# A gated recurrence followed by a max-of-two feed-forward layer: opening reordered, weights prepared in quarters, first casts released chunk by chunk

## The chip, the cores and the metric

The kernel runs on one core of one Trainium2 chip. The metric is the device time of one execution in microseconds (us). A core has these engines: TensorE (PE in the profile; its weight loads are listed apart as PEld), VectorE (DVE), ScalarE (ACT), GpSimd (POOL) and SyncE (SP), which here issues DMAs. Each engine runs its own instructions in program order and waits at semaphores for the others.

## The reference

```python
# x, f_logit: (4, 6144, 256); lower_bound: (256,); all float32
sig = 1.0 / (1.0 + np.exp(-f_logit))
f = lower_bound + (1.0 - lower_bound) * sig
i = 1.0 - f
for t in range(S):                       # S = 6144, h starts at 0 for each of the 4 sequences
    h = f[:, t] * h + i[:, t] * x[:, t]
    y[:, t] = h
X = y.reshape(24576, 256)
g = np.maximum(X @ w1, X @ w2)           # w1, w2: (256, 1024)
out = g @ w_out                          # w_out: (1024, 256)
```

## The kernel before, in words

**Algebra.** With u = sigmoid(-f_logit) and om = 1 - lower_bound, f is 1 - om u and i is om u. The kernel scans y' = f y' + u x, so that y = om y', and puts om into the weights. max(a, b) is a + relu(b - a); so the layer becomes out = relu(y' wd) w_out + y' w13, with wd = om (w2 - w1) and w13 = om (w1 w_out). Both are made in the kernel's opening. Everything that feeds PE is bf16.

**Blocks and chunks.** The 24576 tokens are 48 blocks of 512 (`TB`), 12 to a sequence. Blocks 0 to 2 are loaded as float32 rows, go through sigmoid (`gate_nat`) and product (`drive_nat`) and are transposed by PE (`turn_pe`). All later blocks come in chunks: chunk 0 is block 3 alone, chunk 1 is blocks 4 and 5, chunk 2 is 6 and 7, and so on. `cast(c)` (line 172) has POOL issue two DMAs, fs and xs, that cast the chunk's f_logit and x to bf16 into DRAM scratch; there are `NS` = 3 scratch pairs, taken in turn. `turn_dma(c)` (line 184) has SP issue two DMA transposes from scratch to SBUF, fT and xT. Then `gate(b)` on ACT makes u (line 189), `drive(b)` on DVE makes v = u x (line 200), and for each of the two halves h of the 256 channels DVE makes ff = 1 - om u (`forget`, line 135) and scans (`scan`, line 148).

**The layer.** `hidden(j, fc)` (line 220) makes one of eight groups of 128 hidden units of block j: two matmuls 128x512, one for each half of the channels, into a PSUM tile dT of a pool of five, and a relu that takes it to SBUF as rt, on ACT (line 232) or DVE (line 230). `project(j, slot)` (line 251) is a piece of five matmuls 128x256 into psO (a pool of three): eight steps with rt and w_out, and two with y' and w13. `store` evacuates psO on DVE (line 267) and has SP store it (line 269).

**Order.** It is written out by hand; nothing is planned by a scheduler. In the loop over j (line 466), group fc of block j alternates on PE with a piece of the projection of block j - 1. `gate_at` tells at which (j, fc) the instructions of a block's gate, product and scans are issued: block 3 at (2, 2), 4 at (3, 1), 5 at (3, 5), and b at (b - 2, 4) after that. `turn_of` tells where a chunk's transposes are issued: chunk 0 at (1, 5), 1 at (2, 6), and c at three blocks ahead of its first, group 5. After turn_dma(c) stands cast(c + NS), which waits until its scratch pair was read. SP's one queue holds the loads, then stores and transposes in that order; a transpose that waits holds the stores behind it.

**Opening (lines 366 to 464).** SP issues the loads of blocks 0 to 2 and of the weights, the latter in quarters of w1 and w2 (`weight_load`) and halves of w_out (`wout_load`); ACT issues a first piece of x and lower_bound. PE runs matmuls on a tile of zeros (`keep_warm`). Block 0 is done in two halves of 256 tokens. The weights are prepared in two halves of 512 hidden units: `diff(g)` subtracts on DVE (line 301), `scale(g)` multiplies by om on ACT (line 308), `turn_w1` transposes w1 on PE (line 315), `keep_w1` copies that to SBUF on ACT (line 321), POOL casts w_out to bf16 (lines 423 and 431), and `linear_weights` makes w13 (lines 330 and 339). The eight groups of block 0, its projection and block 1 are woven in between. Then a copy on POOL (line 462) waits for the last load of block 2, and cast(0), cast(1) and cast(2) follow at once.

**Hidden units in a group.** `unit(fc)` takes every fourth of 512 columns; so the weights that PE loads for a group of `wd`, and the columns of w1 that it transposes, lie four elements apart. w_out's rows are loaded to match: one partition gets four rows that follow each other, 4 KB in one piece.

Of the kernel before, what the change touches and what calls it, by code (L numbers as in the profile page):

```python
# [8 lines left out]
FP32 = mybir.dt.float32  # L9
BF16 = mybir.dt.bfloat16  # L10
ALU = mybir.AluOpType
# [5 lines left out]
def kernel(  # L17
# [28 lines left out]
    chunks = [(NP, 1)] + [(j, CB) for j in range(NP + 1, NBLK, CB)]  # L46
    NCH = len(chunks)
    home = {j + o: (c, o) for c, (j, n) in enumerate(chunks) for o in range(n)}
    NS = 3

    const = ctx.enter_context(tc.tile_pool(name="const", bufs=1))
    wpool = ctx.enter_context(tc.tile_pool(name="wpool", bufs=1))
# [155 lines left out]
    HF = DFF // 2  # L208

    def unit(fc):  # L210
        g, q = divmod(fc, 4)
        return slice(g * HF + q, (g + 1) * HF, 4)

    rts = {}

    def hidden(j, fc, on_dve=False):
        y = ys[j]
        dT = ps_d.tile([P, TB], FP32, name="dT")
        for kc in range(KC):
            nc.tensor.matmul(  # L220
                dT[:],
                lhsT=wd[:, kc, unit(fc)],
                rhs=y[:, kc, :],
                start=(kc == 0),
                stop=(kc == KC - 1),
            )
        rt = rpool.tile([P, TB], BF16, name="rt")
        rts[j, fc] = rt
        if on_dve:
            nc.vector.tensor_relu(out=rt[:], in_=dT[:])  # L230
        else:
            nc.scalar.activation(out=rt[:], in_=dT[:], func=AF.Relu)  # L232

    pos = {}

# [51 lines left out]
    def weight_load(k, w, src):  # L287
        cols = slice(k * QF, (k + 1) * QF)
        nc.sync.dma_start(
            out=w[:, :, cols], in_=src[:, cols].rearrange("(h p) f -> p h f", p=P)  # L290
        )

    def wout_load(g):
        nc.sync.dma_start(
            out=won[:, 4 * g : 4 * g + 4, :],
            in_=moe_w_out[g * HF : (g + 1) * HF, :].rearrange("(p q) c -> p q c", q=4),
        )

    def diff(g, eng):
        cols = slice(g * HF, (g + 1) * HF)  # L300
        eng.tensor_tensor(
            out=wdf[:, :, cols], in0=w2n[:, :, cols], in1=w1n[:, :, cols], op=ALU.subtract
        )

    def scale(g):
        cols = slice(g * HF, (g + 1) * HF)
        for h in range(KC):
            nc.scalar.activation(
                out=wd[:, h, cols], in_=wdf[:, h, cols], func=AF.Copy, scale=om[:, h : h + 1]
            )  # L310

    def turn_w1(g, h):
        pt = ps_d.tile([P, TB], FP32, name="dT")
        for q in range(4):
            nc.tensor.transpose(
                pt[:, q * P : (q + 1) * P], w1n[:, h, unit(4 * g + q)], ident[:]
            )
        return pt

    def keep_w1(g, h, pt):  # L320
        nc.scalar.copy(
            out=w1T[:, 4 * g : 4 * g + 4, h * P : (h + 1) * P],
            in_=pt[:].rearrange("p (q d) -> p q d", q=4),
        )

    def linear_weights():
        psw = ps_o.tile([P, 2, D], FP32, name="psO")
        for h in range(KC):
            for fc in range(FC):
                nc.tensor.matmul(  # L330
                    psw[:, h, :],
                    lhsT=w1T[:, fc, h * P : (h + 1) * P],
                    rhs=wob[:, fc, :],
                    start=(h == 0 and fc == 0),
                    stop=(h == 1 and fc == FC - 1),
                    skip_group_check=True,
                )
        for h in range(KC):
            nc.scalar.mul(w13[:, h, :], psw[:, h, :], om[:, h : h + 1])

    idle = ps_o.tile([P, 2, D], FP32, name="psO")

# [7 lines left out]
                stop=True,  # L350
            )

    gate_at = {NP: (2, 2), NP + 1: (3, 1), NP + 2: (3, 5)}
    gate_at |= {b: (b - 2, 4) for b in range(NP + 3, NBLK)}
    gate_of = {}
    for b, at in gate_at.items():
        gate_of.setdefault(at, []).append(b)
    turn_of = {(1, 5): 0, (2, 6): 1}
    turn_of |= {(chunks[c][0] - 3, 5): c for c in range(2, NCH)}

    with tc.manual_schedule():
        for j in range(NP):
            alloc_in(j)


        load(0, 0, 0, 2)
        load(0, 1, 0, 2, nc.scalar)
        nc.scalar.dma_start(out=lbc[:], in_=lower_bound.rearrange("(h p) -> p h", p=P))
        for k in range(2):
            weight_load(k, w1n, moe_w1)  # L370
            weight_load(k, w2n, moe_w2)
# [4 lines left out]
        for k in range(2, 4):  # L376
            weight_load(k, w1n, moe_w1)
            weight_load(k, w2n, moe_w2)
        wout_load(1)
        for q0 in (0, 2):  # L380
            for s in range(2):
                load(1, s, q0, q0 + 2)
        for s in range(2):
            load(2, s, 0, NQ)

        nc.vector.memset(warm[:], 0.0)  # L386
        make_identity(nc, ident[:])
        nc.vector.tensor_copy(out=ident_b[:], in_=ident[:])
        keep_warm(9)


        gate_nat(0, 0, 2)
        drive_nat(0, 0, 2)
        for s in range(2):
            for q in range(2):
                turn_pe(0, s, q)
        nc.vector.tensor_scalar(
            out=om[:], in0=lbc[:], scalar1=-1.0, scalar2=1.0, op0=ALU.mult, op1=ALU.add
        )
        nc.vector.tensor_scalar_add(out=nom[:], in0=lbc[:], scalar1=-1.0)  # L400
        for h in range(KC):
            forget(0, h, 0, HB, on_act=True)
        for h in range(KC):
            scan(0, h, 0, HB)
        keep_warm(3)
        gate_nat(0, 2, 4)
        drive_nat(0, 2, 4)
        for s in range(2):
# [1 line left out]
                turn_pe(0, s, q)  # L410
        for h in range(KC):
            forget(0, h, HB, TB, on_act=True)
        diff(0, nc.vector)
        scale(0)
        pts = [turn_w1(0, h) for h in range(KC)]
        for h in range(KC):
            scan(0, h, HB, TB)
        keep_warm(3)
        for q in range(4):
            hidden(0, q, on_dve=(q % 2 == 1))  # L420
        for h in range(KC):
            keep_w1(0, h, pts[h])
        nc.gpsimd.tensor_copy(out=wob[:, 0:4, :], in_=won[:, 0:4, :])
        for i in range(4):
            project_steps(0, i, 0, 4)
        diff(1, nc.vector)
        scale(1)
        pts = [turn_w1(1, h) for h in range(KC)]
        for q in range(4):
            hidden(0, 4 + q, on_dve=(q % 2 == 1))  # L430
        nc.gpsimd.tensor_copy(out=wob[:, 4:8, :], in_=won[:, 4:8, :])
        for h in range(KC):
            keep_w1(1, h, pts[h])


        gate_nat(1, 0, 2)
        drive_nat(1, 0, 2)
        linear_weights()
        for s in range(2):
            for q in range(2):  # L440
                turn_pe(1, s, q)
# [3 lines left out]
            scan(1, h, 0, HB)  # L445
        gate_nat(1, 2, 4)
        drive_nat(1, 2, 4)
        for i in range(2):
            project_steps(0, i, 4, 8)
        for s in range(2):  # L450
            for q in range(2, 4):
                turn_pe(1, s, q)
# [1 line left out]
            forget(1, h, HB, TB, on_act=True)  # L454
        for h in range(KC):
            scan(1, h, HB, TB)
        for i in range(2, 4):
            project_steps(0, i, 4, 8)
        for i in range(4):
            project_steps(0, i, 8, 10)  # L460

        nc.gpsimd.tensor_copy(out=held[:], in_=ins[2][1][:, NQ - 1, D - 1 : D])
        for c in range(NS):
            cast(c)

        for j in range(1, NBLK + 1):
            if j == 2:
                for slot in range(4):
                    project(1, slot)
            for fc in range(FC):  # L470
                if j < NBLK:
                    hidden(j, fc, on_dve=(j == 1 and fc % 3 == 2))
                if j == 2:
                    if fc % 2:
                        project(1, 4 + fc // 2)
                elif j > 2:
                    project(j - 1, fc)
                if j == 1:
                    if fc == 0:
                        gate_nat(2, 0, NQ)  # L480
                        drive_nat(2, 0, NQ)
                        store(0, 0)
                    if fc == 3:
                        store(0, 1)
                    if fc in (5, 6):
                        for q in range(NQ):
                            turn_pe(2, fc - 5, q)
                    if fc == 7:
                        for h in range(KC):
                            forget(2, h, on_act=True)  # L490
                        for h in range(KC):
                            scan(2, h)
                if fc == 0 and j > 2:
                    store(j - 2, 1)
                if fc == 4 and 1 < j < NBLK:
                    store(j - 1, 0)
                if j == NBLK and fc in (3, 5, 7):
                    if fc == 3:
                        store(j - 1, 0)
                    else:  # L500
                        store_row(j - 1, 1, (fc - 5) // 2)
                for b in gate_of.get((j, fc), []):
                    gate(b)
                    drive(b)
                    for h in range(KC):
                        forget(b, h)
                        scan(b, h)
                c = turn_of.get((j, fc))
                if c is not None:
                    turn_dma(c)  # L510
                    if c + NS < NCH:
                        cast(c + NS)

# [29 lines left out]
```

## Time and profile before

| | |
|---|---|
| median of 4 runs | 413.39 us (412.54 to 413.98) |
| the profiled execution, its device time | 415.36 us |
| its span, from the first to the last instruction | 413.6 us |
| mean granted clock of TensorE in it | 0.982 |
| PE busy | 393.7 us, 95% of the span |
| ACT busy, DVE busy, POOL busy | 272.5, 249.7, 28.4 us |
| DMA | 79.12 MB, mean 191 GB/s |
| first weight load of line 220 for blocks 0, 1, 2, 3, 4, 5 | 11.69, 27.50, 35.35, 43.26, 57.44, 69.17 us |
| POOL issues cast(0), cast(1), cast(2) | 20.49 to 23.28 us |
| SP issues fT of chunks 0, 1, 2 | 33.32, 45.81, 59.99 us |

The profile tells of each instruction when it started and how long it took, and for an idle engine which event ended the wait. The chain of waits follows the work that ended last back from the end. Matmuls are pipelined, so PE's busy time does not say how fast it goes; the start of the same matmul in one block and the next does. A DMA's row gives the time from its issue to its landing. Times below are counted from the span's start.

### The profile page before, as it was taken

How to read it: one execution, taken by the hardware profiler on the slowest of the kernel's cores; microseconds unless marked ns; L12 is line 12 of the kernel's file. 1: busy time of each engine (PE TensorE's matmuls, PEld its weight loads, DVE VectorE, ACT ScalarE, POOL GpSimd, SP SyncE). 2: the span in 40 equal slices, each digit the busy share in tenths (PEclk: the TensorE clock that was granted, in tenths of full speed). 3: DMA queues.
4: the chain of work that ended last, by engine and by line, in shares of the span. 5: the costliest groups of instructions: out<-in, count | busy, mean ns of one | idle time of the engine just before them, and what ended most of it. 6: DMA issues, size and time to landing. Idle time of an engine off the chain costs nothing.

```text
span 413.6 us, 7136 instructions
## 1 busy us (share of the span) xinstructions
PE 393.7 (95%) x2735; PEld 283.0 (68%) x2783; DVE 249.7 (60%) x349; ACT 272.5 (66%) x451; POOL 28.4 (7%) x55
## 2 busy tenths in 40 slices
PE   7988859999999999999999999999999999999996
PEld 3565526777777777777777777777777777777775
DVE  3655466567567567557657657657657657656721
ACT  4665255676776676676676676677677677677662
POOL 0230011001001001001001001001001000000000
PEclk9899968999999999999999999999999999999999
DMA  8999999999999999889889999989989986627112
GB/s 264 345 170 189 172 205 208 229 193 214 216 182 218 180 217 220 176 212 211 209 185 189 227 193 202 207 201 202 206 201 198 212 194 164 148 86 175 52 76 103
DMA packets 125858, 79.12 MB, mean 191 GB/s; under 512 B 96512, under 2 KB 101888, under 8 KB 125824
## 3 DMA queue, kind: packets, MB, share of 16 engines
q1 hardware_dynamic: 113024, 54.80, 52.1%
q0 software_dynamic: 12256, 23.60, 35.2%
q8 instruction: 22, 0.36, 0.3%
q10 hardware_dynamic: 544, 0.26, 0.2%
q14 instruction: 12, 0.10, 0.1%
HBM read 53.48 MB, written 48.76 MB: 247 GB/s over the span
## 4 chain that ended last, share of the span: by engine, by line
PE 84%; DMA 3%; DVE 2%; SPq 1%; issue 1%; ACT 0%; DVEq 0%
PE psO L251 47%; PE dT L220 36%; DMA fT<-fs 2%; DVE y L148 1%; SPq L184 1%; DMA xT<-xs 1%; DVE osb L267 0%; DMA out_dram<-osb 0%; DVE v L200 0%; DVE ff L135 0%; ACT u L189 0%; SPq L269 0%; DVE rt L230 0%; ACT osb L277 0%; DVEq L200 0%
## 5 line engine op out<-in xcount | busy, mean ns | idle before, releaser
L232 ACT ACTIVATE rt<-dT 128x512 bf16<-128x512 f32 x378 | 219.6, 597 | 118.4 <-PE dT L220 116.3
L251 PE MATMUL psO<-wob,rt 128*128 128x256 bf16 x1536 | 230.9, 274 | 0.6 <-DVE rt L230 0.2
L220 PE MATMUL dT<-y,wd 128*128 128x512 bf16 x720 | 219.0, 383 | 10.4 <-DVE y L148 4.0
L251 PEld LDWEIGHTS <-rt 128*128 128x128 bf16 x1536 | 150.9, 98 | 94.9 <-issue 4.9
L148 DVE TENSOR_TENSOR_SCAN y<-ff,y,v 128x512 bf16<-128x512 bf16 x84 | 107.8, 1284 | 3.0
L267 DVE COPY osb<-psO 128x512 f32<-128x512 f32 x95 | 64.4, 679 | 68.4 <-PE psO L251 68.4
L220 PEld LDWEIGHTS <-wd 128*128 128x128 bf16 x768 | 85.6, 114 | 16.0 <-issue 5.1
L200 DVE TENSOR_TENSOR v<-u,xT 128x1024 bf16<-128x1024 bf16 x45 | 31.1, 692 | 71.4 <-ACT u L189 60.4
L251 PE MATMUL psO<-w,y 128*128 128x256 bf16 x384 | 73.3, 274 | 0.0
L189 ACT ACTIVATE u<-fT 128x1024 bf16<-128x1024 bf16 x45 | 47.2, 1050 | 6.3 <-DMA fT<-fs 6.3
L251 PEld LDWEIGHTS <-y 128*128 128x128 bf16 x384 | 37.8, 98 | 4.5
L135 DVE TENSOR_SCALAR ff<-u,nom 128x512 bf16<-128x512 bf16 x90 | 30.5, 339 | 0.0
L172 POOL DMA_DIRECT2D fs<-in_f_logit_dram x23 | 12.7, 553 | 254.8 <-DMA fT<-fs 254.8
L172 POOL DMA_DIRECT2D xs<-in_x_dram x23 | 12.8, 558 | 31.5 <-DMA xT<-xs 31.0
L148 DVE TENSOR_TENSOR_SCAN y<-ff,y,dT 128x256 bf16<-128x256 bf16 (+1 forms) x8 | 6.6, 866 | 2.8 <-ACT ff L131 2.8
L110 DVE TENSOR_TENSOR vn<-un,xn 128x512 bf16<-128x512 bf16 (+1 forms) x5 | 4.0, 793 | 6.7 <-ACT un L103 6.5
L345 PE MATMUL psO<-warm 128*128 128x512 bf16 x15 | 6.6, 600 | 1.2 <-DVE warm L386 1.2
L148 DVE TENSOR_TENSOR_SCAN y<-ff,v 128x512 bf16<-128x512 bf16 x6 | 7.3, 1225 | 0.2
L230 DVE TENSOR_SCALAR rt<-dT 128x512 bf16<-128x512 f32 x6 | 4.1, 689 | 4.1 <-PE dT L220 4.1
L131 ACT ACTIVATE ff<-dT,nom 128x256 bf16<-128x256 bf16 (+1 forms) x10 | 4.6, 515 | 2.6 <-DVE nom L400 1.6
L345 PEld LDWEIGHTS <-warm 128*128 128x128 bf16 x15 | 2.0, 143 | 3.8 <-issue 2.5
L103 ACT ACTIVATE un<-fn 128x512 bf16<-128x512 f32 (+1 forms) x5 | 3.6, 721 | 1.5 <-DMA fn<-in_f_logit_dram 1.5
(29 smaller groups left out, 33.0 us busy)
## 6 DMA issues: line engine op xcount, KB each, us to landing
out_dram<-osb SPq DMA_DIRECT2D x95, 256.0 KB, 2.9
fs<-in_f_logit_dram POOLq DMA_DIRECT2D x22, 512.0 KB, 6.6
xs<-in_x_dram POOLq DMA_DIRECT2D x22, 512.0 KB, 8.1
fn<-in_f_logit_dram SPq DMA_DIRECT2D x4, 256.0 KB, 5.6
w1n<-in_moe_w_dram SPq DMA_DIRECT2D x4, 256.0 KB, 5.6
w2n<-in_moe_w_dram SPq DMA_DIRECT2D x4, 256.0 KB, 5.6
won<-in_moe_w_out_dram SPq DMA_DIRECT2D x2, 512.0 KB, 6.3
xn<-in_x_dram SPq DMA_DIRECT2D x3, 256.0 KB, 6.0
```

Source lines behind the costliest of these rows:

```text
L131: nc.scalar.activation(out=o, in_=i, func=AF.Identity, bias=1.0, scale=nom[:, h : h + 1])
L135: nc.vector.tensor_scalar(out=o, in0=i, scalar1=nom[:, h : h + 1], scalar2=1.0, op0=ALU.mult, op1=ALU.add)
L148: nc.vector.tensor_tensor_scan(out=ys[j][:, h, t0:t1], data0=ffs[j][:, h, t0:t1], data1=vT[j][:, h, t0:t1], initial=initial, op0=ALU.mult, ...
L172: nc.gpsimd.dma_start(out=t[0 : n * TB, :], in_=src[b, k * TB : (k + n) * TB, :], max_dma_last_dim=4096,)
L184: nc.sync.dma_start_transpose(out=t[:, :, 0:n], in_=rows[c][s][0:n, :])
L189: nc.scalar.activation(out=us[j][:], in_=chunk[c, 0][:, :, o * TB : (o + 1) * TB], func=AF.Sigmoid, scale=-1.0,)
L200: nc.vector.tensor_tensor(out=vT[j][:], in0=us[j][:], in1=chunk[c, 1][:, :, o * TB : (o + 1) * TB], op=ALU.mult,)
L220: nc.tensor.matmul(dT[:], lhsT=wd[:, kc, unit(fc)], rhs=y[:, kc, :], start=(kc == 0), stop=(kc == KC - 1),)
L232: nc.scalar.activation(out=rt[:], in_=dT[:], func=AF.Relu)
L251: nc.tensor.matmul(ps, lhsT=lhsT, rhs=rhs, start=(s == 0 and (r == 0 or alone)), stop=(s == FC + KC - 1 and (r == 1 or alone)), skip_group ...
L267: nc.vector.tensor_copy(out=osb[:], in_=pos[j, g, 0][:])
L345: nc.tensor.matmul(idle[:].rearrange("p r d -> p (r d)"), lhsT=warm[:, 0:P], rhs=warm[:], start=True, stop=True,)
```

## The change

1. `unit(fc)` takes 128 columns that follow each other. w_out is loaded to match: four rows of 1 KB for a partition, 128 rows apart.
2. The weights are prepared in quarters of 256 hidden units. `diff` takes a quarter k and a range of channel halves: quarter 0 is subtracted by POOL, quarter 1 half by POOL and half by DVE, quarters 2 and 3 by DVE. `scale` of quarters 0, 2 and 3 goes to POOL, of quarter 1 stays on ACT. `turn_w1` and `keep_w1` take a quarter, and `linear_weights` is made in two parts.
3. The opening is reordered. POOL issues the load of lower_bound first; om and nom are made ahead of the first product; one of the first two forget pieces goes to DVE; the first two groups of block 0 are made in two halves of tokens; the first half of block 1 is loaded ahead of w_out's second half; the projection of block 0 goes by steps over its four tiles. In block 1 four relus go to DVE (odd groups) where two did.
4. The first casts: the copy on POOL waits for block 1's last load. cast(0) follows, and turn_dma(0) is issued right there, ahead of all stores. A new copy on POOL, `wait_turned`, waits for chunk 0's xT, then cast(1) is issued. At (2, 5) turn_dma(1) is issued, `wait_turned(1)`, then cast(2) and cast(3). `NS` is 2, so later cast(c + 2) follows turn_dma(c).
5. Block 6's gate moves from (4, 4) to (4, 7).

```diff
-    NS = 3
+    NS = 2
...
     def unit(fc):
-        g, q = divmod(fc, 4)
-        return slice(g * HF + q, (g + 1) * HF, 4)
+        return slice(fc * P, (fc + 1) * P)
...
+    def hidden_cols(j, fc, t0, t1):
+        if t0 == 0:
+            dts[j, fc] = ps_d.tile([P, TB], FP32, name="dT")
         for kc in range(KC):
             nc.tensor.matmul(
-                dT[:],
+                dts[j, fc][:, t0:t1],
                 lhsT=wd[:, kc, unit(fc)],
-                rhs=y[:, kc, :],
+                rhs=ys[j][:, kc, t0:t1],
...
-            in_=moe_w_out[g * HF : (g + 1) * HF, :].rearrange("(p q) c -> p q c", q=4),
+            in_=moe_w_out[g * HF : (g + 1) * HF, :].rearrange("(q p) c -> p q c", p=P),
...
+    def diff(k, h0, h1, eng):
+        cols = slice(k * QF, (k + 1) * QF)
         eng.tensor_tensor(
-            out=wdf[:, :, cols], in0=w2n[:, :, cols], in1=w1n[:, :, cols], op=ALU.subtract
+            out=wdf[:, h0:h1, cols],
+            in0=w2n[:, h0:h1, cols],
+            in1=w1n[:, h0:h1, cols],
+            op=ALU.subtract,
+        )
+
+    def scale(k, h, on_pool=False):
+        cols = slice(k * QF, (k + 1) * QF)
+        if on_pool:
+            nc.gpsimd.tensor_scalar_mul(
+                out=wd[:, h, cols], in0=wdf[:, h, cols], scalar1=om[:, h : h + 1]
+            )
+            return
+        nc.scalar.activation(
+            out=wd[:, h, cols], in_=wdf[:, h, cols], func=AF.Copy, scale=om[:, h : h + 1]
+        )
...
-    gate_at = {NP: (2, 2), NP + 1: (3, 1), NP + 2: (3, 5)}
-    gate_at |= {b: (b - 2, 4) for b in range(NP + 3, NBLK)}
+    gate_at = {NP: (2, 2), NP + 1: (3, 1), NP + 2: (3, 5), NP + 3: (4, 7), NP + 4: (5, 4)}
+    gate_at |= {b: (b - 2, 4) for b in range(NP + 5, NBLK)}
...
-    turn_of = {(1, 5): 0, (2, 6): 1}
+    turn_of = {(2, 5): 1}
     turn_of |= {(chunks[c][0] - 3, 5): c for c in range(2, NCH)}
+
+    def wait_turned(c):
+        nc.gpsimd.tensor_copy(out=held[:], in_=chunk[c, 1][:, KC - 1, chunks[c][1] * TB - 1 :][:, 0:1])
...
+        nc.gpsimd.dma_start(out=lbc[:], in_=lower_bound.rearrange("(h p) -> p h", p=P))
         load(0, 0, 0, 2)
         load(0, 1, 0, 2, nc.scalar)
-        nc.scalar.dma_start(out=lbc[:], in_=lower_bound.rearrange("(h p) -> p h", p=P))
...
+        for s in range(2):
+            load(1, s, 0, 2)
         wout_load(1)
-        for q0 in (0, 2):
-            for s in range(2):
-                load(1, s, q0, q0 + 2)
+        for s in range(2):
+            load(1, s, 2, 4)
         for s in range(2):
             load(2, s, 0, NQ)
...
+        diff(0, 0, KC, nc.gpsimd)
+        turn_w1(0)
+        keep_warm(4)
         gate_nat(0, 2, 4)
         drive_nat(0, 2, 4)
...
         for h in range(KC):
             forget(0, h, HB, TB, on_act=True)
-        diff(0, nc.vector)
-        scale(0)
-        pts = [turn_w1(0, h) for h in range(KC)]
+            scale(0, h, on_pool=True)
+        for fc in range(2):
+            hidden_cols(0, fc, 0, HB)
+        keep_w1(0)
+        diff(1, 0, 1, nc.gpsimd)
         for h in range(KC):
             scan(0, h, HB, TB)
-        keep_warm(3)
...
+        turn_w1(1)
+        diff(1, 1, 2, nc.vector)
+        for h in range(KC):
+            scale(1, h)
         nc.gpsimd.tensor_copy(out=wob[:, 0:4, :], in_=won[:, 0:4, :])
...
+        for fc in range(2):
+            hidden_cols(0, fc, HB, TB)
+            relu(0, fc, on_dve=(fc == 1))
+        for fc in range(2, 4):
+            hidden(0, fc, on_dve=(fc == 3))
+        keep_w1(1)
+        diff(2, 0, KC, nc.vector)
+        for h in range(KC):
+            scale(2, h, on_pool=True)
+        for s in range(4):
+            for i in range(4):
+                project_steps(0, i, s, s + 1)
+        turn_w1(2)
+        keep_w1(2)
+        diff(3, 0, KC, nc.vector)
+        for h in range(KC):
+            scale(3, h, on_pool=True)
+        for fc in range(4, 6):
+            hidden(0, fc, on_dve=(fc == 5))
+        linear_weights(0, 4)
+        turn_w1(3)
+        for fc in range(6, 8):
+            hidden(0, fc, on_dve=(fc == 7))
         nc.gpsimd.tensor_copy(out=wob[:, 4:8, :], in_=won[:, 4:8, :])
...
-        nc.gpsimd.tensor_copy(out=held[:], in_=ins[2][1][:, NQ - 1, D - 1 : D])
-        for c in range(NS):
-            cast(c)
+        nc.gpsimd.tensor_copy(out=held[:], in_=ins[1][1][:, NQ - 1, D - 1 : D])
+        cast(0)
+        turn_dma(0)
+        wait_turned(0)
+        cast(1)
...
-                    hidden(j, fc, on_dve=(j == 1 and fc % 3 == 2))
+                    hidden(j, fc, on_dve=(j == 1 and fc % 2 == 1))
...
                 if c is not None:
                     turn_dma(c)
+                    if c == 1:
+                        wait_turned(1)
+                        cast(2)
                     if c + NS < NCH:
                         cast(c + NS)
```

## The prediction

> **What bounds the kernel now.** I read, in this order, the page's slices, the busy time by stages, the chain of waits in order of time, and the DMA issues cut to single windows. TensorE (PE) is the bound from block 5 on. The first weight load of line 220 starts at 69.17 us for block 5 and at 397.61 for block 47, so a block takes (397.61 − 69.17)/42 = 7.82 us, and no block between them differs. From 69.17 to the end of the span (413.6) everything runs at that pace. Before 69.17 it does not: columns below are PE, PEld, DVE, ACT, POOL busy, granted clock, DMA share, GB/s.
>
> ```profile
> 45.00:50.00 5.00, 4.95 (x36) 3.63 (x36) 0.95 (x2) 1.19 (x2) 0.00 (x0) 1.00 1.24 170
> 50.00:55.00 5.00, 2.10 (x15) 1.36 (x14) 0.00 (x0) 2.08 (x4) 0.55 (x1) 0.92 1.03 239
> 55.00:60.00 5.00, 3.20 (x12) 1.33 (x11) 4.81 (x7) 3.21 (x6) 0.67 (x1) 0.50 1.08 157
> 60.00:65.00 5.00, 4.78 (x21) 2.85 (x20) 3.80 (x6) 1.42 (x3) 0.00 (x0) 0.55 1.13 215
> 100.00:150.00 50.00, 49.63 (x353) 36.46 (x359) 33.19 (x46) 34.80 (x57) 3.29 (x6) 1.00 1.02 207
> ```
>
> PE stands idle about 4.7 us from 50 to 60, and then runs at half clock until about 64.5; block 4 takes 69.17 − 57.44 = 11.73 us for 7.82. The chain of waits says what it stood for (start, length, what):
>
> ```profile
> 45.81 4.77 SPq L184
> ...
> 50.68 4.34 DMA xT<-xs
> ...
> 55.12 0.69 DVE v L200
> 55.81 0.27 DVE ff L135
> 56.08 0.02 issue
> 56.10 1.28 DVE y L148
> 57.39 0.26 DVE ff L135
> 57.65 0.02 issue
> 57.67 1.29 DVE y L148
> 58.97 0.04 issue
> 59.01 0.59 PE dT L220
> ```
>
> Chunk 1 (blocks 4, 5) is turned late. From the landing of xT (55.02) to PE's second matmul of block 4 (59.01) is 4.0 us of DVE. So **every block's start is a race between PE and "xT landed + 4.0"**, and the whole change is worth what it takes off the last block that loses this race. Three DMA rows carry the forecast: fT of chunk 1 (issued 45.81), fT and xT of a late chunk (152.74, 154.34).
>
> ```profile
> fT<-fs SPq DMA_TRANSPOSE x1, 7.1
> ```
> ```profile
> fT<-fs SPq DMA_TRANSPOSE x1, 4.5
> xT<-xs SPq DMA_TRANSPOSE x1, 5.2
> ```
>
> The first ran beside a cast: chunk 3's xs was issued at 41.25 and took 8.8, to 50.0. It landed at 52.9, 2.9 after that. The next two turns repeat it: fT at 65.9 with the cast done at 63.0, and 80.8 with 77.5, 2.9 and 3.3 after; xT each time 5.0 to 5.3 after. A turn issued beside a cast ends as if it began when the cast was done. Alone, a pair takes 154.34 + 5.2 − 152.74 = 6.8.
>
> **The change, step by step.** I follow it to PE's second matmul of blocks 1, 2, 3, 4, 6.
>
> *Block 1 (27.6 before).* The subtract of half the weights (1.22 us at 9.66 on DVE) no longer stands ahead of block 0's second scans: they end at 9.6 + 1.38 = 11.0, not 12.2. Then DVE subtracts its eighth (1.22/4 = 0.3). POOL's cast of the output weights (1.04, at about 10.95 as now) is beside it, and the old row shows what that does: the same subtract took 1.22 alone and 1.86 with that cast beside it. I let it end at 12.3. Scale 0.42 on ACT gives 12.75; hidden units 2 and 3 (four matmuls, 0.86) and the second relu on DVE (0.69) give 14.4; subtract of the third quarter 0.61, 15.05; POOL's two scales, 15.65. POOL's prices are not in the trace: its cast of 1024 elements took 1.04, so 256 scaled cost 0.26 to 0.52, and a subtract of 512 with two inputs 0.52 to 1.04; I take 0.3 and 1.04. The first subtract starts at 6.9 (w2n's first landing) and has until 9.5, so both ends are hidden. From 15.7 PE is the pace: units 4, 5 (0.86), eight w13 matmuls (0.87), transposes (0.5), units 6, 7 (0.86), 18.8. Block 1's first sigmoid waits in ACT's order for a relu, 19.1, where it stood at 21.16. From it to block 1 is 27.5 − 21.16 = 6.3, kept. **Block 1 at 25.4**, with 24.5 if no subtract is blocked and 27.5 if nothing is gained.
>
> The Trainium skill's "GPSIMD Engine Reference", section 3.1, speaks against moving subtracts to POOL: about 2.6 cycles an element for two inputs, an estimate of 1.1 us for 512. By it the sum stays as it is, since that subtract has 2.6 us of room.
>
> *Block 2 (37.08).* DVE gets four relus of block 1 in place of two, all ahead of block 2's scan. Now it is 4.76 from the product's start (29.82) to the scan (34.58), with 1.1 of waiting; then 1.23 + 2 × 0.69 + 4 × 0.69 = 5.4. Loss 0.7: 9.6 + 0.7 after block 1, **35.7**.
>
> *Block 3 (44.83).* Now 7.75 after block 2, of which ACT waited 0.24 for fT; then 7.5, if chunk 0 is turned. It is: the gate is now block 1's last load (about 17.6) and not block 2's (20.3); cast(0) took 5.5 from its issue (20.49) to its last landing, the remaining 1 MB of loads adds up to 1, so 24.3; a pair of half size another 3.5, 28. **43.2**.
>
> *Block 4 (59.01).* cast(1) now waits for that, 28; 0.5 MB of a cast took 2.5 in the burst (landings 29.0, 31.5, 34.0), and a first one 4.9 to 6.2, so it is done by 37. SP issues turn(1) behind store(1, 0), which DVE evacuates after block 3's scans: 45.81 − 44.83 = 1.0 after block 3, now and then: 44.2. No cast runs beside it any more: 6.8, so xT at 51.0 for 55.0; + 4.0, **55.0**. Gate 5 has its data at the same time.
>
> *Block 6 (77.1).* The new wait ends at 51.0, and behind it in POOL's queue stand cast(2) **and** cast(3): four pieces, issued from 51.4. First piece 5.6, three at 2.5, one store in between 0.6: done at 65.1. SP issues turn(2) when piece 1 has landed (57.0), and by the rows above it ends 2.9 (fT) and 5.0 (xT) after the burst: 68.0 and 70.1. Gate 6, moved from (4, 4) to (4, 7), lets PE run through block 4 and, with five dT buffers, half of block 5 while ACT waits for fT. + 4.0: **74.1**, against 55.0 + 15.64 = 70.6 by PE. The gain at block 6 is 3.0.
>
> *Clock.* Before, the half clock from 59.0 to 64.5 cost 5.5/2 = 2.7, which 77.1 holds. Afterwards PE idles about 2.8 in pieces around 69 to 74. Nothing to 2.7; I take 1.0, since the gap is in pieces.
>
> *After that* nothing: chunk 3 is turned by 84 and needed at 86; a cast fires two chunks ahead (31 us) and needs 11, its turn 7.
>
> *Costed at nothing.* Contiguous slices: the wd load takes 114 ns and the rt load 98 (page), but five projections start in 0.54 (65.80 to 66.34), 0.109 each, the load of wd included; it lies under matmuls. If the 16 ns were on the path it would be 16 × 16 × 47 = 12 us, and no row says so. wout in 1 KB pieces: two 256 KB loads with such pieces land 0.66 apart, 1.3 for 1.2. lower_bound by POOL first: it landed 4.7 after issue on ACT; 4.2 to 4.7 from POOL gives 4.6 to 5.7, so the first product (4.76) can be 0.9 late, which ends in the wait for x's second half (8.2).
>
> Sum: the profiled execution has 413.6 of span in 415.36 (1.8 around it); the median shown is 413.39. 3.0 − 1.0 = 2.0 off: span 411.6, profiled 413.4, median **411.4**.
>
> **Rivals.**
>
> *Turns share with the casts* (0.27). If fT of chunk 2 moves between the pieces, it takes the 7.1 of the one row that overlapped most: 57.0 + 7.1 + 2.1 + 4.0 = 70.2, PE's own 70.6 decides. Gain 6.5, less a clock dip of 1.7 or none: 407.8. For it: stores issued beside casts land in 5.3 to 5.8, not 2.3 to 2.9, late but not last. Against: three turns out of three.
>
> The Trainium skill's "DMA: Bandwidth & Descriptors", section "Queues, rings and completion order", says that an engine takes turns between queues, a packet each. By that rule a turn would get a packet in after each piece of the burst, and the sum goes towards this rival; the measured rows are with a single piece left, so they can't decide between the two.
>
> *The burst is dearer* (0.15, slower). Pairs of casts among stores took 9.6 (53.42 to 62.98) to 11.0. If two cost 9.6 each, the burst ends at 51.4 + 19.2 = 70.6, xT lands at 75.6 and block 6 starts at 79.6: 2.5 late, and 1.0 of clock, 416.9. It decides once xT(2) lands after 73.1. For it: DMA share over 1 in this stage. Against: the first burst, with little beside it, kept 2.5 a piece.
>
> *The opening gains nothing* (inside my case, 0.58): POOL's pieces and blocked subtracts eat the 2.1; then block 6 starts at 76.2 and the time is 413.5, no change.
>
> **Numbers.** Forecast 0.58 (of it faster 0.34, same 0.18, slower 0.06), sharing 0.27 (0.26, 0.01, 0), burst 0.15 (0, 0.01, 0.14). About 0.3% (1.2 us) is what a measurement can tell from no change. Faster 0.60, same 0.20, slower 0.20. Range 406.4 to 415.0: it reaches the sharing case without a dip (406.9) and leaves out most of the dear burst.
>
> **What would show it.** Block 1's first wd load near 25.4; turn(1) issued near 44 and landed in about 7; four cast issues in a row near 51; fT(2) landing 3 after the last of them. Block 6 near 70.6 speaks for sharing, at 79 for the burst; a block period other than 7.82 would make all of it wrong.

## The result, and the profile after

The changed kernel took 414.77 us (median of 44 executions, 412.63 to 416.70) against 412.93 for before (63 executions, 411.21 to 416.07): ratio 1.0041, 95% interval 1.003 to 1.0052, so 0.4% slower where I had forecast 0.5% faster. Yet its profiled execution (414.17, span 412.4) is shorter than that of before (415.36, span 413.6). Both facts need a cause.

The busy time by stages of the changed kernel, the same windows as for before (columns: window, length, busy time of PE, PEld, DVE, ACT, POOL, granted clock, DMA share, GB/s):

```profile
45.00:50.00 5.00, 4.95 (x37) 3.51 (x37) 0.49 (x1) 1.06 (x3) 0.00 (x0) 1.00 0.84 194
50.00:55.00 5.00, 2.85 (x17) 1.40 (x15) 2.82 (x5) 4.90 (x8) 2.83 (x5) 0.95 0.63 149
55.00:60.00 5.00, 4.05 (x15) 2.23 (x15) 4.93 (x7) 1.20 (x2) 0.00 (x0) 0.50 1.08 183
60.00:65.00 5.00, 4.78 (x32) 3.32 (x32) 1.55 (x3) 2.54 (x5) 0.00 (x0) 0.87 1.12 229
100.00:150.00 50.00, 49.63 (x354) 35.05 (x360) 32.61 (x46) 34.94 (x58) 3.31 (x6) 1.00 1.03 207
```

The last row has the pace of before: a block still takes 7.82 us. The half clock ends at 61.3 (0.87 in the fourth row), where before had it until 64.4 (0.55). PE still idles between 50 and 57, and the chain of waits (start, length, what) says that a second wait has come behind it:

```profile
47.37 4.64 DMA xT<-xs
...
52.14 0.02 POOL held L383
52.16 0.63 issue
52.78 4.97 DMA fs<-in_f_logit_dram
57.76 0.02 issue
57.77 5.21 SPq L184
...
63.07 8.61 DMA xT<-xs
...
71.78 0.69 DVE v L200
...
75.53 0.68 DVE osb L275
76.21 0.04 issue
76.25 0.70 PE psO L259 x5
```

xT of chunk 1 lands at 52.02 and lets the copy of `wait_turned(1)` go (L383); behind it POOL issues the casts of chunks 2 **and** 3 (52.78 to 54.41, landed at 57.76, 60.68, 64.02 and 66.97). SP has issued turn(2) at the first landing, but its issue of fT takes 5.21 us (1.93 for turn(1), with no cast beside it), and xT then takes 8.61. The two turns by their DMA rows (operation, count, median us from issue to landing), turn(1) with no cast beside it, then turn(2) beside the burst:

```profile
fT<-fs SPq DMA_TRANSPOSE x1, 4.6
xT<-xs SPq DMA_TRANSPOSE x1, 4.6
```
```profile
fT<-fs SPq DMA_TRANSPOSE x1, 10.8
xT<-xs SPq DMA_TRANSPOSE x1, 8.6
```

fT lands 1.6 and xT 4.7 after the last cast. The opening did not gain anything: block 1's first weight load stands at 27.53, for 27.50 before. GpSimd's instructions in it (start, length, what, idle before):

```profile
7.64 1.28 POOL L309 TENSOR_TENSOR wdf<-w2n,w1n 128x512 f32<-128x512 f32 x1 [4.89 <-DVE vn L110]
9.02 1.97 POOL L319 TENSOR_SCALAR wd<-wdf,om 128x256 bf16<-128x256 f32 x2
10.96 0.72 POOL L309 TENSOR_TENSOR wdf<-w2n,w1n 128x256 f32<-128x256 f32 x1
...
16.39 4.00 POOL L319 TENSOR_SCALAR wd<-wdf,om 128x256 bf16<-128x256 f32 x4 [3.69 <-DVE wdf L309]
20.35 1.03 POOL L475 CAST wob<-won 128x1024 bf16<-128x1024 f32 x1
21.33 0.18 POOL L509 COPY held<-xn 128x1 f32<-128x1 f32 x1
```

One scaling of 256 elements (L319) takes 1.00 us on average (0.91 to 1.29), and the cast of 1024 only 1.03. The last four end at 20.4, and the copy that releases cast(0) stands behind them: cast(0) is issued at 21.45, 1.0 later than before, though the load it waits for had landed at 18.46.

### The profile page after: what moved, and what is told of

Same layout as the page of the kernel before. It is cut to its first block, busy times and chain, and to the rows that moved or that the text cites. A ratio compares the mean times of both kernels' runs of the same rounds, so it can differ in the third digit from the quotient of the medians.

```text
span 412.4 us, 7153 instructions
## 1 busy us (share of the span) xinstructions
PE 392.2 (95%) x2736; PEld 273.2 (66%) x2784; DVE 249.1 (60%) x353; ACT 269.2 (65%) x446; POOL 39.1 (9%) x66
## 4 chain that ended last, share of the span: by engine, by line
PE 81%; DMA 4%; DVE 3%; SPq 2%; issue 2%; ACT 1%; DVEq 0%; POOL 0%; POOLq 0%
PE psO L259 46%; PE dT L221 35%; DMA xT<-xs 3%; SPq L184 2%; DVE y L148 1%; DMA fs<-in_f_logit_dram 1%; DVE osb L275 1%; DVE rt L234 0%; DVE v L200 0%; DVE vn L110 0%; DVE ff L135 0%; ACT un L103 0%; ACT u L189 0%; ACT rt L236 0%; PE dT L122 0%
## 5 line engine op out<-in xcount | busy, mean ns | idle before, releaser
L236 ACT ACTIVATE rt<-dT 128x512 bf16<-128x512 f32 x376 | 218.1, 598 | 118.0 <-PE dT L221 115.4
L221 PE MATMUL dT<-y,wd 128*128 128x512 bf16 (+1 forms) x724 | 219.0, 381 | 11.2 <-DVE y L148 3.8
L221 PEld LDWEIGHTS <-wd 128*128 128x128 bf16 x772 | 75.7, 99 | 18.8 <-issue 2.9
L234 DVE TENSOR_SCALAR rt<-dT 128x512 bf16<-128x512 f32 x8 | 5.3, 688 | 4.9 <-PE dT L221 4.9
L366 PE MATMUL psO<-warm 128*128 128x512 bf16 x12 | 5.5, 632 | 1.2 <-DVE warm L411 1.2
L319 POOL TENSOR_SCALAR wd<-wdf,om 128x256 bf16<-128x256 f32 x6 | 6.0, 1001 | 3.8 <-DVE wdf L309 3.7
L122 PE MATMUL dT<-ident_b,vn 128*128 128x128 bf16 x24 | 2.6, 250 | 2.8 <-DVE vn L110 2.6
```

The costliest lines, as they stand in the source:

```text
L221: nc.tensor.matmul(dts[j, fc][:, t0:t1], lhsT=wd[:, kc, unit(fc)], rhs=ys[j][:, kc, t0:t1], start=(t0 == 0 and kc == 0), stop=(t1 == TB an ...
L236: nc.scalar.activation(out=rt[:], in_=dts[j, fc][:], func=AF.Relu)
L319: nc.gpsimd.tensor_scalar_mul(out=wd[:, h, cols], in0=wdf[:, h, cols], scalar1=om[:, h : h + 1])
L366: nc.tensor.matmul(idle[:].rearrange("p r d -> p (r d)"), lhsT=warm[:, 0:P], rhs=warm[:], start=True, stop=True,)
```

## The experiments

Three theories. **O**: GpSimd's scalings and its load of lower_bound ate the opening's gain. **B**: the burst of casts in front of turn(2) costs what the earlier release gained. **P**: the profiled execution of before is one of its long ones, so that a sum made against it promises too much. All ratios are to the kernel before, timed beside each, with 95% intervals. The first weight load of block 9 is a good ruler: in every profile, what follows it takes 313.1 to 313.2 us. The columns "block 1" and "block 9" give the first weight load of these blocks in the one profiled execution. Block 1 starts at 26.5 to 28.0 in the six profiles with the old opening, and at 26.8 to 28.7 in the four with the new one as it is.

| kernel | median us | ratio | block 1 | block 9 |
|---|---|---|---|---|
| before, profiled for the prediction | | 1 | 27.50 | 100.45 |
| before again (b_again, one execution) | 416.31 | | 27.99 | 101.00 |
| before again (b_timed) | 412.36 | 1.0011 (0.9989 to 1.0033) | 27.70 | 98.42 |
| changed | 414.77 | 1.0041 (1.003 to 1.0052) | 27.53 | 99.17 |
| scale_act | 412.96 | 1.0012 (0.9989 to 1.0035) | 25.65 | 97.41 |
| lbc_act | 414.20 | 1.0023 (1.0002 to 1.0045) | 26.80 | 99.44 |
| open_fix | 412.92 | 1.0004 (0.9991 to 1.0018) | 23.96 | 98.35 |
| gate_only | 414.73 | 1.0054 (1.0033 to 1.0074) | 26.50 | 99.55 |
| open_only | 412.13 | 0.999 (0.9978 to 1.0002) | 26.81 | 97.24 |
| contig | 412.96 | 1.0004 (0.9986 to 1.0022) | 26.89 | 97.16 |
| cast3_late | 415.10 | 1.0064 (1.0035 to 1.0094) | 28.66 | 105.13 |
| no_burst | 411.55 | 0.9963 (0.9943 to 0.9984) | 27.08 | 95.88 |
| one_only | 406.22 | 0.9832 (0.9812 to 0.9852) | 27.85 | 91.32 |
| one_ahead | 402.55 | 0.9765 (0.9742 to 0.9787) | 24.02 | 87.45 |

**b_again and b_timed: the kernel before, unchanged.**

> The kernel before, unchanged, for a second profile of it. Theory P (the profile on which the forecast stood was a slow execution: 415.4 us against a median of 412.9): here block 4 again starts late, near 57.5 to 59, because chunk 1 is turned beside chunk 3's cast, but the stretch at half clock behind it is shorter than 10.2 us, and the second matmul of block 6 comes near 75 and not at 77.1; the span is near 411.2. Rival: every execution has block 6 at 77.1 and the rest of the time lies elsewhere; then the span is about 411 with block 6 unchanged, and the block period is shorter than 7.82.

> The kernel before, unchanged, timed in rounds so that every run lists its span and granted clock. Its two profiled executions took 415.36 and 416.31 us, above its median of 412.93, while the changed kernel's profiled execution (414.17) lies just below its own (414.77). Theory P (the profiled executions of before are its late ones: half clock of 10.2 us and block 6 at 77): most timed runs have spans near 411 at a clock above 0.982, and those near 414 have 0.982 or less. Theory Q (the time is lost outside the span, or the clock has nothing to do with it): span is always the time less 1.8, and clock and time show no tie. Ratio 1.000 within 0.002 by both.

The first took 416.31 us, again with 10.2 us at half clock: that single execution did not bear P out. The second settles it by its times. Its profiled execution took 413.47 us; of the windows that had 0.50 and 0.55 for a clock in the prediction's profile it says:

```profile
55.00:60.00 5.00, 3.23 (x13) 1.55 (x12) 4.89 (x9) 2.96 (x5) 0.58 (x1) 0.50 1.07 179
60.00:65.00 5.00, 4.95 (x33) 3.34 (x32) 3.90 (x5) 2.39 (x4) 0.00 (x0) 0.90 1.07 213
```

Half clock lasts from 54.2 to 61.0 here, 6.8 us for 10.2, and block 9 starts 2.0 us earlier. The executions of before that list their clock put it beyond doubt: 77 of 93 ran at 0.990 or more, with medians of 412.4 us (71 of them, up to 0.992) and 412.1 (six above); ten at 0.986 to 0.988 have a median of 413.65, and six at 0.982 or 0.983 have 415.4. Both profiles I had were of the rarest kind, and that of b_timed (0.988) is of the middle one. Of the changed kernel's 44, 41 ran at 0.990 or more, its profiled one (0.992) among them. What lies around the span is 1.7 to 2.9 us in these, 1.9 as a median, and 1.8 in the changed kernel, so the difference is not there: theory Q of b_timed's expectation is out.

The stretches at half clock in the loop last 10.2, 10.2, 6.8 and 6.8 us in these profiles (before three times, changed once), and 3.4 or 6.8 in others below: one, two or three times 3.4. The Trainium skill's "TensorE: Matmul & The Clock Gate", section "What's actually happening", says that the gate judges TensorE's activity in free-running windows of 3.4 us. The runs agree, in that like waits do not cost alike. contig, below, is before with its slices changed; its wait for block 4 ends as in b_timed (second matmul at 58.39, for 58.38), but the clock stays full:

```profile
55.00:60.00 5.00, 2.56 (x19) 1.53 (x17) 4.89 (x9) 3.20 (x6) 0.59 (x1) 1.00 1.09 177
```

Its only half clock in the loop lies behind block 3's wait, from 46.1 to 49.5, and block 5 starts at 65.88, for 67.14 in b_timed. That the place of the waits in the windows decides this is the page's reading; no run here moves it alone.

**scale_act, lbc_act, open_fix: the opening's parts back on ScalarE.**

```diff
-            scale(0, h, on_pool=True)
+            scale(0, h)
...
-        nc.gpsimd.dma_start(out=lbc[:], in_=lower_bound.rearrange("(h p) -> p h", p=P))
         load(0, 0, 0, 2)
         load(0, 1, 0, 2, nc.scalar)
+        nc.scalar.dma_start(out=lbc[:], in_=lower_bound.rearrange("(h p) -> p h", p=P))
```

scale_act has the first (for quarters 0, 2 and 3), lbc_act the second, open_fix both.

> The changed kernel with the six scalings that POOL makes (1.0 us each) on ACT (0.5 us each in this kernel's profile). Theory O: the stretch from the third quarter's subtract (15.6) to POOL's cast of the output weights' second half (20.35) shrinks by about 2 us, block 1 starts near 25.5 and not 27.5, and since every later step up to block 6 hangs on block 1, the time falls by 1.5 to 2 us. Rival (block 1's own loads or ACT's order set its start): block 1 moves by less than 0.5, the time by less than 0.5.

> The changed kernel with lower_bound loaded on ACT's queue behind x, as before, and not first on POOL. Theory O (the opening lost to POOL what it won): lower_bound lands near 5.9 and not 6.8, the first product starts at 4.8 and not 7.0, the first scan near 6.3 and not 8.35; of these 2 us, at most 0.5 to 1 reach block 1 (27.5), since POOL's scalings of 1.0 us each bound the stretch from 16.4 to 20.4: 0.5 to 1 us less time. Rival (the scalings alone set block 1): block 1 stays within 0.3 of 27.5 and the time is that of the changed kernel.

> The changed kernel with lower_bound's load and all six scalings on ScalarE, its casts as they are. The two cures of the opening gave 0.6 and 1.8 us one by one; if they add up: block 1 near 25, xT(1) near 49.5, the four casts from 50.3 to 64.5, xT(2) near 69, block 6 at 73 to 73.5, 2.2 to 2.7 less than the changed kernel, 412.0 to 412.5, ratio 0.998 to 1.000. So the opening that I had forecast would make the change no loss and no gain against the usual execution of before. Rival (the cures overlap, one wait hides the other): that of the scalings alone, 413.

O holds for the scalings. With the scalings on ACT, block 1 starts at 25.65 (1.9 earlier), cast(0) is issued at 18.32 instead of 21.45, and block 6's second matmul stands at 73.91, for 75.67. The time falls by 0.3% with it (ratio 1.0012, for 1.0041; the intervals just touch). Their row in scale_act, with the two of quarter 1:

```profile
L323 ACT ACTIVATE wd<-wdf,om 128x256 bf16<-128x256 f32 x8 | 3.7, 504 | 0.7 <-DVE wdf L309 0.7
```

That is half of GpSimd's 1.00 us a piece. And the load of lower_bound: GpSimd issues it at 1.27 and it lands at 6.79; ACT issues it at 1.23 and it lands at 5.66. VectorE makes om from it, ahead of its first product, which starts at 6.96 in the changed kernel and at 5.83 in lbc_act. The row of om, first in the changed kernel, then in lbc_act:

```profile
6.81 0.17 DVE L418 TENSOR_SCALAR om<-lbc 128x2 f32<-128x2 f32 x1 [3.81 <-DMA lbc<-in_lower_bound_dram]
```
```profile
5.68 0.17 DVE L418 TENSOR_SCALAR om<-lbc 128x2 f32<-128x2 f32 x1 [4.12 <-DMA lbc<-in_lower_bound_dram]
```

What this load costs by itself is not shown: lbc_act's block 1 (26.80) is no earlier than that of open_only (26.81), which has the load on GpSimd, and its ratio's interval reaches from 1.0002 to 1.0045.

With both cures block 1 starts at 23.96, 1.7 before scale_act's, but the time hardly follows: 412.92, for 412.96 with the scalings alone, so the rival of open_fix's expectation is right in its number. The burst is where it goes. Against scale_act, xT(1) is 0.9 earlier (49.30), and xT(2) only 0.2 (69.70), since the burst took 14.9 us for 14.2; then blocks 6, 7 and 8 start 9.13, 9.05 and 8.98 us after the block before, 1.7 more in all than in scale_act. The chain of open_fix shows what holds them:

```profile
60.78 8.92 DMA xT<-xs
...
73.55 0.68 DVE osb L275
74.23 0.04 issue
74.27 0.70 PE psO L259 x5
74.98 0.30 PE dT L221 x2
75.28 6.48 DMA fT<-fs
...
81.86 1.06 ACT u L189
82.92 1.47 ACT rt L236 x3
```

The turn after the burst comes late, too: fT(3) is issued at 75.28, when PE has gone on, and lands at 81.76. ACT waits for it in program order, and the relus that stand behind it (L236) hold PE.

**gate_only, open_only, contig: the change in its parts.** gate_only is the opening of before with parts 4 and 5 of the change, open_only its parts 1 to 3 with the casts of before, contig its part 1 alone.

> The opening of before with the changed kernel's casts: two scratch pairs, cast(0) released by block 1's last load, waits on chunks 0 and 1, block 6's gate at (4, 7). Theory B (what the change loses comes from the burst of cast(2) and cast(3) ahead of turn(2)): block 1 at 27.5 as in both kernels, turn(1) issued near 45.3, the four cast issues from 52.5, xT(2) near 71.5, block 6 at 75.5, and the time that of the changed kernel, 414.0 to 415.0, ratio 1.003 to 1.005. Rival (the new opening itself loses, by its relus on VectorE and pieces on GpSimd): the time of before, 412.9, or less.

> The changed kernel's opening (contiguous slices, quarters, lower_bound by GpSimd) with the casts of before: three scratch pairs, three casts at once behind block 2's last load, turn(0) at (1, 5), turn(1) at (2, 6), block 6's gate at (4, 4). Theory B: block 1 at 27.5, cast(0) issued near 21.5, turn(1) beside the third cast, block 4's second matmul 58 to 59.5, block 6 near 77, time of before, 412.5 to 413.5, ratio 0.999 to 1.001. Rival (the opening itself loses): 414 to 415.

> The kernel before with part 1 of the change alone: 128 neighbouring columns for a group, w_out in pieces of 1 KB. The load of wd takes 99 ns for 114 in the changed kernel, and a block 7.82 us in both. If the load lies under matmuls, as I forecast: 7.82 a block and the time of before, ratio 0.998 to 1.002. If it is on the path: up to 12 us less (16 loads of 16 ns in 47 blocks), ratio 0.97.

The loss is in the casts: gate_only has all of it (1.0054), open_only none (0.999). Part 5 is in gate_only too, but no_burst and one_ahead, below, keep it and lose nothing. In gate_only, the cast issues start at 51.58, xT(2) lands at 70.88, and blocks 6, 7 and 8 start 9.72, 9.03 and 9.01 after the block before, with the same wait for fT(3) as in open_fix. Contiguous slices are worth nothing, as forecast. The page of contig has their load at 98 ns, for 114 before, and the block at 7.82:

```profile
L219 PEld LDWEIGHTS <-wd 128*128 128x128 bf16 x768 | 74.9, 98 | 18.3 <-DVE y L148 4.4
```

**cast3_late, no_burst: what the burst costs.** The first holds back chunk 3's cast until chunk 2 is turned. The second has one scratch pair, so that every cast after cast(2) goes out behind the turn before it; opening, waits and turn(1) stay.

```diff
-                    if c == 1:
-                        wait_turned(1)
-                        cast(2)
-                    if c + NS < NCH:
+                    if c in (1, 2):
+                        wait_turned(c)
+                        cast(c + 1)
+                    if 1 < c < NCH - NS:
                         cast(c + NS)
```
```diff
-    NS = 2
+    NS = 1
...
                         wait_turned(1)
-                        cast(2)
```

> The changed kernel with chunk 3's cast held until chunk 2's turn has landed; so one cast and not two stands ahead of turn(2). Theory B (the burst sets block 6): fT of chunk 2 lands about 3 us after a burst that ends near 61 and not 67, so near 64 instead of 68.6, xT near 66 instead of 71.7; block 6 then starts when PE is done with block 5, near 74.0, and not at 75.7: 1.5 to 2 us less than the changed kernel (ratio to the kernel before near 1.000). Rival (turns move between the casts' pieces, so the burst costs nothing): block 6 stays at 75.7 and the time within 0.5 us. If chunk 3 becomes late in turn (two casts now stand ahead of turn(3)), block 8 shows it, later than 91.35.

> The changed kernel with one scratch pair: after chunk 1 only cast(2) is issued ahead of turn(2), and each later cast behind the turn before it, so that no two casts stand ahead of a turn; opening, waits and turn(1) at (2, 5) are left. It prices the burst apart from the late turn(1). Theory B: block 4 at 56 as in the changed kernel, cast(2) from 52.8 to 60.5, xT(2) by 66 to 68.5, block 6's second matmul where PE lets it, 72 to 74, and blocks 7 and 8 at 7.82 behind it; 1.5 to 2.5 us less than the changed kernel, 412.3 to 413.3, ratio 0.999 to 1.002. Rival (the two waits on GpSimd set the time, the burst does not): block 6 at 75 or later and 414 to 415.

In cast3_late, xT(2) lands at 68.47 although block 1 came 1.1 later, and block 6 follows block 5 by 7.81. But cast(3) and cast(4) are now issued together at 69.24 to 70.87: the burst has moved by one chunk. It ends at 84.04, fT(3) lands 1.9 after that, and PE stands before block 8. So the kernel gained nothing by it: 1.0064, where I had expected 1.000. The windows are those of its profiled execution, which at 420.27 us was the longest of the twelve, so only the order of events is read from them:

```profile
80.00:85.00 5.00, 3.26 (x22) 2.06 (x21) 0.00 (x0) 0.00 (x0) 0.00 (x0) 1.00 1.16 240
85.00:90.00 5.00, 2.22 (x7) 0.95 (x8) 2.26 (x4) 3.49 (x6) 1.22 (x2) 0.72 1.14 256
```

no_burst takes the burst away and leaves the rest. turn(2), issued at 56.99 with one cast still running to 60.31, needs:

```profile
fT<-fs SPq DMA_TRANSPOSE x1, 6.2
xT<-xs SPq DMA_TRANSPOSE x1, 4.4
```

xT(2) lands at 65.30, and from block 5 on every block takes 7.82. The time is 411.55, 0.9963 of before, where the changed kernel has 1.0041: by these two ratios the burst costs 0.78%, 3.2 us, more than the 1.5 to 2.5 I had expected. Without it, the change is a small gain even with its spoilt opening. Of the 3.3 us between the two profiles at block 9, 1.5 are there at block 5 already: no_burst's opening happened to be 0.5 earlier, and its half clock behind block 4's wait lasted 3.4 us for 6.8. So the price goes by the times of all executions and not by this pair.

**one_only, one_ahead: casts one chunk ahead.** one_only has the opening and the gates of before, one_ahead those of open_fix; their casts against the changed kernel's are

```diff
-    NS = 2
+    NS = 1
...
-    turn_of = {(2, 5): 1}
+    turn_of = {(1, 7): 1}
...
         cast(0)
         turn_dma(0)
-        wait_turned(0)
         cast(1)
...
                     turn_dma(c)
-                    if c == 1:
-                        wait_turned(1)
-                        cast(2)
                     if c + NS < NCH:
                         cast(c + NS)
```

> The opening of before, unchanged, with casts that go one chunk ahead: one scratch pair, cast(0) behind block 1's last load, turn(0) at once, cast(c + 1) behind turn(c), turn(1) at (1, 7). It parts the 9.6 us that the last such kernel gained between the opening and the casts. Theory B (the casts are nearly all of it): block 1 at 27.5 or a little earlier, cast(1) landed by 37, turn(1) at 43 to 44, so that blocks 4 and 6 wait for nothing, block 6 at 66.5 to 68, no half clock; time 404.5 to 406, ratio 0.981 to 0.985, the opening being worth the other 2 to 3 us. Theory O alone (the opening is the larger part): 408 or more.

> The changed kernel with lower_bound's load and all six scalings on ScalarE, and a cast that goes ahead of no turn but its own: one scratch pair, cast(c + 1) behind the issue of turn(c), so that it waits for that turn's read; turn(1) at (1, 7); no copy that waits for a turn. Theory B with O (opening worth 2 us, a burst in front of a turn worth the rest): block 1 near 25, xT(0) near 27.5, cast(1) from 27.5 to 37, turn(1) landed at 44 to 45, so block 4 waits no longer than PE, 49 to 50.5; cast(2) from 44.5 to 54, xT(2) by 63, block 6 at 65.5 to 66.5; no half clock; span 402 to 404, time 404 to 406, ratio 0.978 to 0.984. Rival (the chip's DMA needs the late casts: a cast beside block 2's gate and the stores takes longer than 10): block 4 at 53 or later and a gain under 1%. Rival (something other than block 6's start sets the end): block 6 near 66 and a time over 410.

The windows of one_ahead:

```profile
50.00:55.00 5.00, 4.95 (x38) 3.53 (x37) 3.22 (x5) 3.04 (x6) 0.44 (x1) 1.00 1.16 231
55.00:60.00 5.00, 4.95 (x38) 3.53 (x37) 2.40 (x4) 3.83 (x7) 0.67 (x2) 1.00 1.12 230
60.00:65.00 5.00, 5.00 (x39) 3.52 (x37) 4.93 (x8) 3.86 (x7) 0.00 (x0) 1.00 0.93 225
```

PE is busy throughout at full clock; from block 4 (48.35) every block takes 7.82. 402.55 us (four executions) is 2.35% less than before (2.1 to 2.6). It goes on from the change's own idea, an early first cast, but turn(1) is issued 13 us earlier (32.23, for 45.34) and nothing but a turn's own cast stands ahead of it. one_only (five executions) has 6.7 of these 9.6 us with the old opening. So the cured opening, with parts 1 and 5, is worth 2.9 us once the turns are in time, and about 2 while they are not (open_fix 1.0004, gate_only 1.0054).

## Why the prediction was wrong

*Block 1 at 25.4* failed: 27.53. The step "its cast of 1024 elements took 1.04, so 256 scaled cost 0.26 to 0.52" took a cast for a scaling; the row says 1.00 on average, so the six cost 6.0 us of GpSimd's time for 1.8. The range was made of one row's own scaling up and down, no bound at all for another operation. Second, lower_bound: "4.2 to 4.7 from POOL gives 4.6 to 5.7", but the issue started at 1.27 and the landing took 5.5, to 6.79. Third, and small, the subtract of 512 took 1.28 (taken as 1.04), and waited for VectorE's product until 7.64; it had room, as I had said. The Trainium skill's "GPSIMD Engine Reference", section 3.1, from which the prediction had an estimate of 1.1 for it, was nearer than my 1.04.

*From block 1 to block 6 the chain was right.* scale_act is the test, since its block 1 (25.65) is nearly what I forecast: block 6's second matmul 73.91, forecast 74.1. In the changed kernel itself: the pair of turn(1) 6.7 (forecast 6.8); block 4 at xT + 4.0 (56.00); burst 14.2 us from its first issue to its last landing (13.7); fT and xT of chunk 2 1.6 and 4.7 behind it (2.9 and 5.0); block 6 at xT + 4.0 (75.67). The loss of 0.7 in block 2 did not show: its second matmul stands at 37.07, 9.54 behind block 1's first weight load, for 9.58 before.

*Clock* was mis-sized: I took 1.0 us for PE's idle pieces after block 6 and got 0.4 (block 7's second matmul at 83.85, 8.18 behind block 6's). The 77.1 that I compared with was, besides, the first matmul of block 6; its second stands at 77.31. So the span is 1.6 over the forecast at block 6 and 0.8 under it by the rest, 412.4 for 411.6. Against the profiled execution of before the sum was off by 0.8 only. And one term was put at nothing without a reason: block 4's own wait. PE ran at half clock from 54.46 to 61.29 behind it, and block 5 starts 11.63 after block 4, for 7.82; so "70.6 by PE" was 74.2 in this execution, and even without the burst (no_burst) block 6's second matmul stands at 72.75.

*The sum itself* failed, and by more: "the profiled execution has 413.6 of span in 415.36 (1.8 around it); the median shown is 413.39", and I took the 2.0 between them off both kernels. But that excess was half clock that 77 of 93 executions of before do not have, and the changed kernel's do not have it either: its median is 0.6 above its profiled execution. 2.0 + 0.6 + 0.8 is the 3.4 us between 411.4 and 414.77. In the step's words, "the half clock from 59.0 to 64.5 cost 5.5/2 = 2.7, which 77.1 holds"; but a usual execution has less of it. No profile of before itself is a usual one; its median (412.4), less 1.9 around the span, 313.1 from block 9 on and three blocks of 7.82, puts the first weight load of block 6 at 73.9, an estimate, and the profiles of contig and open_only, which have the casts of before and a clock of 0.992, have its second matmul at 74.02 and 73.99. So a block 6 at 74.1 had nothing to gain, not 3.0. scale_act shows what would have become of the forecast with its opening: 412.96, no change.

*The rivals.* "Turns share with the casts" fell as a price: the turn landed behind the burst (10.8 and 8.6, for 4.6 and 4.6 with no cast beside it). Yet the queues do take turns, as the Trainium skill's "DMA: Bandwidth & Descriptors", section "Queues, rings and completion order", says. What the changed kernel's queues moved (queue, kind: packets, MB, share of 16 engines; q0 has the casts, q1 here the transposes), from 63 to 66 us in the burst and from 67 to 68 behind it:

```profile
q0 software_dynamic: 278, 0.54, 94.2%
q1 hardware_dynamic: 275, 0.07, 17.3%
```
```profile
q1 hardware_dynamic: 1150, 0.29, 127.7%
```

Packet for packet the turn got as many as the casts. But one of its packets is 256 bytes (0.07 MB in 275) and one of theirs mostly 2 KB, so it moved 0.02 MB in a us beside them and 0.29 alone. So it ends nearly as if it began when the casts were done. (From 58 to 60 q1 moved nothing at all, though fT had been issued at 57.77; what held it then stays open.) The prediction's "a packet in after each piece of the burst" counted pieces of 0.5 MB where the turns go by packets.

"The burst is dearer" fell as a price (14.2 for 13.7), but its place was right: what turned the gain into a loss is the burst in front of turn(2), 3.2 us by no_burst. "The opening gains nothing" came true, and I had put it inside my case, at 413.5; the missing 1.3 is again the baseline (2.6, of which a smaller loss at block 6 and behind it gave 1.3 back).

*Still open:* why the changed kernel's executions differ by 4 us (412.63 to 416.70) at nearly one clock, and so why its median lies above its profiled execution. In gate_only, open_fix and lbc_act, blocks 7 and 8 came late as well; that this happens in some executions of the changed kernel is argued, not shown.

## What to carry to other kernels

A staged transfer is only early if nothing else is issued ahead of its second stage: two casts ahead of a turn put the turn behind both. With the opening of before, casts one chunk ahead and an earlier turn gained 1.7% (one_only) where two casts ahead lost 0.5% (gate_only). Before a sum is made against a profiled execution, see whether that execution is a usual one: its time against the median, and its granted clock against that of the other executions. And where an engine has no row for an operation, a cheaper operation's row is no upper bound: ask what is lost if it costs several times as much.

## What the runs showed of the hardware that I had not expected

- GpSimd multiplies 256 elements a partition by a scalar of that partition in 1.00 us (mean of six in the changed kernel, 0.91 to 1.29), and casts 1024 in 1.03: 3.9 against 1.0 ns an element. ScalarE takes 0.50 for the former.
- The load of 256 single floats landed 5.5 us after GpSimd's issue (0.88 of it issuing) in the changed kernel and 4.4 after ScalarE's (0.52) in lbc_act; 5.2 to 5.7 and 4.3 to 5.0 over all the profiles.
- The two copies of one element a partition that only wait for a turn took GpSimd 1.18 and 0.71 us in the changed kernel, 0.19 and 0.71 in scale_act.
- Behind a burst of casts SP's issue of fT takes 5.2 to 7.2 us (the latter in cast3_late); it took 1.9 for the changed kernel's turn(1), with no cast beside it, and 4.7 in one_ahead beside the last piece of one cast. So a part of the turn's delay is already in its issue.
- Beside casts the DMA engines served the two queues packet for packet, 275 and 278 in 3 us, so the transpose with its packets of 256 bytes got an eighth of the casts' bytes.
